# Computing the first MLP matrix product of the last chunk with seven block products instead of eight

## The chip, the core and the metric

The kernel runs on one core of a Trainium2 chip. The metric is the device time of one execution in microseconds (us); less is better. A core has a matrix engine (TensorE, PE in the profile; its weight loads are shown apart as PEld), a vector engine (VectorE, DVE), a scalar engine (ScalarE, ACT), a general engine (GpSimd, POOL) and SyncE (SP), which here only issues transfers. Each engine works through a queue of its own, in the order of the program, and waits for the others by semaphores. Matrix products land in eight PSUM banks of 512 float32 values in each of 128 partitions; everything else lies in SBUF.

## The reference, cut to what matters

```python
# retention: q, k, v are (4, 8, 768, 64)
for t in range(S):
    state = gamma * state + einsum('bhd,bhe->bhde', k[:, :, t], v[:, :, t])
    y[:, :, t] = scale * einsum('bhd,bhde->bhe', q[:, :, t], state)
x = y.transpose(0, 2, 1, 3).reshape(3072, 512)
# MLP: w_in is (512, 2048), w_out is (2048, 512)
h = x @ w_in
c = sqrt(2 / pi)
g = 0.5 * h * (1 + tanh(c * (h + 0.044715 * h**3)))
return g @ w_out
```

## The kernel before, in words

The 768 steps are cut into six chunks of 128 steps (0 to 5). For each chunk and each of four batches the attention part makes x, stored transposed as `xT[c]`: model dimension on the partitions (four tiles `kc` of 128), 4 x 128 tokens along the free axis. Then comes the MLP of these 512 tokens in two stages.

M1 is h = x @ w_in. `moe1(c, fc)` makes one of 16 tiles of 128 columns of w_in: `moe1_mm` (L348) runs four matmuls of 512 tokens, one for each `kc`, into an "h" bank, and `gelu` (L364) on ACT writes the tile in float16 to `g_sb`. There are two "h" banks, two "o" banks and four "att" banks.

M2 is g @ w_out. It is already done with seven products for eight. The 16 tiles are taken as eight pairs `fp` (r = 0 or 1 in a pair), the tokens as a half b = 0 or 1 (twice, a = 0 or 1), the outputs as halves x = 0 or 1. `g_sums` makes four sums of blocks of g (`s_g[1]` to `s_g[4]`), `w_sums` four of w_out (`t_w[1]` to `t_w[4]`), both through `tt` (L387). `PROD` lists seven products; `units_w(c)` runs them in 14 units, (product, a), each of eight matmuls of 256 columns (L456). X and Z name two banks. The partial sums are copied out between products (`SNAP`, to s_p, s_u, s_q, L479) and added to later banks on DVE (`ADD`, L387), and blocks of the output are stored. In the last chunk, 5, each half a has its own bank, X and Z in "o" and "h" banks, and the stores are cut finer.

```python
PROD = (
    ("X", (0, 0), (0, 0), True, False),
    ("Z", (1, 0), (1, 0), True, True),
    ("X", 2, 2, False, False),
    ("Z", 1, 1, True, False),
    ("X", 3, 3, False, False),
    ("Z", 4, (1, 1), False, True),
    ("X", (1, 1), 4, False, True),
)
```

A tuple names a block, a number one of the four sums; `True, False` say that a bank is begun and that it is ended.

The order on every engine is written out by hand. `run(units, after)` runs a list of units and after unit i what `after[i]` names. For chunks 2 to 5 the units are 16 of M1 and then 14 of M2 (so unit 16 is the first of M2). In between stand the attention work of the next chunk (n = c + 1), the loads of the one after (m = c + 2, issued by SP after unit 0), and the sums of g after units 3, 7, 11 and 15: on POOL in chunks 2 to 4, on DVE in chunk 5. In chunk 4 the attention of chunk 5 ends after unit 25.

The load buffers have tags "q32" and "k32" (eight each) and "v32" (six); each holds 2 KB in a partition. The whole of w_in lies in SBUF in four tiles `w_in_sb[0]` to `w_in_sb[3]`, of four `fc` each.

Of the kernel before, what the change touches and what calls it, by code (L numbers as in the profile page):

```python
# [9 lines left out]
F16 = mybir.dt.float16  # L10
F32 = mybir.dt.float32
AF = mybir.ActivationFunctionType
ALU = mybir.AluOpType
# [3 lines left out]
def kernel(  # L17
# [9 lines left out]
    nc = tc.nc  # L27
    B, H, S, Dh = q.shape
    C = 128
    NCk = S // C  # L30
# [3 lines left out]
    NF = d_ff // 128  # L34
# [23 lines left out]
    ld = ctx.enter_context(tc.tile_pool(name="ld", bufs=2 * B))  # L58
    pre = ctx.enter_context(tc.tile_pool(name="pre", bufs=2 * B))
    att = ctx.enter_context(tc.tile_pool(name="att", bufs=4))  # L60
    xp = ctx.enter_context(tc.tile_pool(name="xp", bufs=1))
    gp = ctx.enter_context(tc.tile_pool(name="gp", bufs=1))
# [27 lines left out]
    def load(c):  # L90
# [20 lines left out]
        out=misc[:, 0:1], in_=zero[:, 0:1], func=AF.Gelu_apprx_tanh, scale=1.0  # L111
# [15 lines left out]
    for j in range(2):  # L127
        for hp in range(NHP):
            nc.vector.tensor_scalar(
                out=mask[:, j, hp],  # L130
                in0=cst[:, OT:OT + 128],
# [8 lines left out]
    def copy_on(eng, out, in_):  # L140
        if eng is nc.scalar:
            eng.copy(out=out, in_=in_)  # L142
        else:
            eng.tensor_copy(out=out, in_=in_)
# [26 lines left out]
    xT = {}  # L171
# [4 lines left out]
    def bank(tag, dt=F32, shape=(128, NHP, 128), name="ps"):  # L176
        return psum.tile(list(shape), dt, tag=tag, bufs=BANKS[tag], name=name)
# [120 lines left out]
    def att_AY(c, bs, tag, ca, abs_, eng):  # L298
# [20 lines left out]
    w_in_sb = [  # L319
        const.tile([128, NHP, n * 128], F16, name=f"w_in{i}") for i, n in enumerate(w_in_n)  # L320
    ]
    w_in_of = {
        at + r: (i, r) for i, (n, at) in enumerate(zip(w_in_n, w_in_at)) for r in range(n)
    }
# [18 lines left out]
    g_sb = {}  # L343

    def moe1_mm(c, fc, out, t0, t1):
        wi, wr = w_in_of[fc]
        for kc in range(NHP):
            nc.tensor.matmul(  # L348
                out=out,
                lhsT=w_in_sb[wi][:, kc, wr * 128:(wr + 1) * 128],  # L350
                rhs=xT[c][:, kc, t0:t1],
                start=(kc == 0),
                stop=(kc == NHP - 1),
                skip_group_check=True,
            )

    def g_tile(c, fc):
        if (c, fc // 8) not in g_sb:
            g_sb[c, fc // 8] = gp.tile([128, 8, B * C], F16, tag=f"g{fc // 8}", name="g")
        r = fc % 8 // 2 * 2  # L360
        return g_sb[c, fc // 8][:, r:r + 2]

    def gelu(out, in_):
        nc.scalar.activation(out=out, in_=in_, func=AF.Gelu_apprx_tanh, scale=1.0)  # L364

    def moe1(c, fc):
        h_ps = bank("h", shape=(128, B * C), name="h_ps")
        moe1_mm(c, fc, h_ps, 0, B * C)
        gelu(g_tile(c, fc)[:, fc % 2], h_ps)
# [11 lines left out]
    s_g = {i: const.tile([128, NP, 2, C], F16, name=f"s_g{i}") for i in (1, 2, 3, 4)}  # L381
# [4 lines left out]
    def tt(eng, out, in0, in1, op):  # L386
        eng.tensor_tensor(out=out, in0=in0, in1=in1, op=op)  # L387
# [5 lines left out]
        tt(nc.vector, t[2], w_q(i, 1, 1), t[1], ALU.subtract)  # L393
        tt(nc.vector, t[4], w_q(i, 1, 0), t[2], ALU.subtract)

    def g_sums(eng, c, f0, f1, p0=0, p1=2):
        g = g_sb[c, f0 // 4].rearrange("p (f r) (a b t) -> p r b f a t", r=2, a=2, b=2)
        i = f0 % 4
        q = {
            (r, b): g[:, r, b][:, i:i + f1 - f0, p0:p1] for r in range(2) for b in range(2)  # L400
        }
        t = {j: s_g[j][:, f0:f1, p0:p1] for j in s_g}
        tt(eng, t[1], q[0, 1], q[1, 1], ALU.add)
        tt(eng, t[2], t[1], q[0, 0], ALU.subtract)
        tt(eng, t[3], q[0, 0], q[0, 1], ALU.subtract)
        tt(eng, t[4], q[1, 0], t[2], ALU.subtract)

    def lhs(c, key, fp, a):
        if key in s_g:
            return s_g[key][:, fp, a]  # L410
        r, b = key
        b = 2 * a + b
        return g_sb[c, fp // 4][:, 2 * (fp % 4) + r, b * C:(b + 1) * C]

    def rhs(key, fp):
        if key in t_w:
            return t_w[key][:, fp]
        r, x = key
        return w_out_sb[fp // 2][:, 2 * (fp % 2) + r, x * hw:(x + 1) * hw]

    PROD = (
        ("X", (0, 0), (0, 0), True, False),
# [7 lines left out]
    SNAP = {0: "s_p", 2: "s_u", 3: "s_q"}  # L434

    ADD = {1: (0, 0, "s_p"), 4: (1, 1, "s_q"), 5: (0, 1, "s_u")}

    def units_w(c):
        ps, o_sb, snap = {}, {}, {}
        last = c == NCk - 1  # L440

        def bank_of(k, a, new):
            if new:
                if last:
                    ps[k, a] = bank(("o", "h")[a], shape=(128, 2, hw), name="o_ps")[:, 0]
                else:
                    if a == 0:
                        ps[k] = bank("o", shape=(128, 2, hw), name="o_ps")
                    ps[k, a] = ps[k][:, a]
            return ps[k, a]  # L450

        def mm(n, a):
            k, lk, rk, new, stop = PROD[n]
            po = bank_of(k, a, new)
            for fp in range(NP):
                nc.tensor.matmul(  # L456
                    out=po,
                    lhsT=lhs(c, lk, fp, a),
                    rhs=rhs(rk, fp),
                    start=(new and fp == 0 and (last or a == 0)),  # L460
                    stop=(stop and fp == NP - 1),
                    skip_group_check=True,
                )

        def o_tile(b):
            if b not in o_sb:
                o_sb[b] = op.tile([128, 2, d_model], F32, tag=f"o{b}", name="o_sb")
            return o_sb[b]

        def snap_tile(nm):  # L470
            if nm not in snap:
                snap[nm] = op.tile([128, 2, hw], F32, tag=nm, name=nm)
            return snap[nm]

        def ev(n, a0, a1):
            k = PROD[n][0]
            p = ps[k, a0].unsqueeze(1) if last else ps[k]
            if n in SNAP:
                nc.scalar.copy(out=snap_tile(SNAP[n])[:, a0:a1], in_=p)  # L479
            elif n in ADD:  # L480
                b, x, nm = ADD[n]
                o = o_tile(b)[:, a0:a1, x * hw:(x + 1) * hw]
                tt(nc.vector, o, p, snap[nm][:, a0:a1], ALU.add)
            else:
                nc.scalar.copy(out=o_tile(1)[:, a0:a1, 0:hw], in_=p)  # L485

        def store(b, a0, a1, n0, n1, eng):
            rows = out.rearrange("(a b t) n -> b t a n", a=2, b=2)
            eng.dma_start(  # L489
                out=rows[b, c * C:(c + 1) * C, a0:a1, n0:n1], in_=o_sb[b][:, a0:a1, n0:n1]  # L490
            )

        def unit(n, a):
            mm(n, a)
            if not last:
                if a == 1:
                    ev(n, 0, 2)
                    if n > 4:
                        store(n - 5, 0, 2, 0, d_model, nc.gpsimd)
            elif n < 6:  # L500
                ev(n, a, a + 1)
                if n == 4 and a == 1:
                    store(1, 1, 2, hw, d_model, nc.sync)
                if n == 5:
                    store(0, a, a + 1, 0, d_model, (nc.scalar, nc.sync)[a])
            elif a == 0:
                ev(n, a, a + 1)
                store(1, 0, 1, 0, d_model, nc.scalar)
            else:
                nc.scalar.copy(out=o_tile(1)[:, 1, 0:hw], in_=ps["X", 1])  # L510
                store(1, 1, 2, 0, hw, nc.sync)

        return [(lambda n=n, a=a: unit(n, a)) for n in range(7) for a in range(2)]

    def units_0():
        ps, snap = {}, {}
# [91 lines left out]
    def run(units, after):  # L608
        for i, u in enumerate(units):
            u()  # L610
            for f, *args in after.get(i, ()):
                f(*args)

    VE, AC, PO, SY = nc.vector, nc.scalar, nc.gpsimd, nc.sync
# [173 lines left out]
    for c in range(2, NCk):  # L788
        n, m = c + 1, c + 2
        after = {} if n == NCk else {  # L790
            12: [(att_AY, n, (), "att", n, (0, 1), None)],
            19: [(att_AY, n, (0, 1), "h", n, (2, 3), VE)],
            22: [(att_S, n, 0, 1)],
            25: [(att_AY, n, (2, 3), "h", n, (), AC), (att_S, n, 2, 3)],
        }

        def more(at, *what):
            after[at] = after.get(at, []) + list(what)

        for i in range(4):  # L800
            at = 4 * i + 3
            after[at] = [(g_sums, PO if n < NCk else VE, c, 2 * i, 2 * i + 2)] + after.get(at, [])
        if m < NCk:
            more(0, (load, m))
            for b in range(B):
                more((18, 20, 23, 26)[b], (prep_qk, m, b))
                more(24, (prep1, PO, "v", m, b))
        run([(lambda fc=fc: moe1(c, fc)) for fc in range(NF)] + units_w(c), after)


# [28 lines left out]
```

## Time and profile before

| | |
|---|---|
| median of three timed runs | 207.29 us (206.85 to 207.32) |
| the profiled execution's own time | 206.68 us |
| its span, first to last instruction | 204.9 us |
| TensorE clock granted | 1.000 |
| PE busy | 196.4 us, 96% |
| DVE busy | 103.1 us, 50% |
| ACT busy | 102.2 us, 50% |
| POOL busy | 121.9 us, 60% |
| M1 of chunk 5, from the span's start | 175.23 to 189.17 us |
| M2 of chunk 5 | 189.17 to 201.60 us |

The span is what the trace covers; the 1.8 us between it and the execution's time lie around it. "Busy" is the time in which an engine worked on an instruction. Instructions of one engine overlap at their ends, so the mean length of one is more than its share of a dense row: a matmul of 256 columns is shown as 273 ns long while the next starts 109 ns after it. The timeline gives start, length, engine, line, operation and what it writes and reads, and in brackets the idle time ahead of it with what ended that. The chain of waits follows the last instruction back to what released each step.

### The profile page before, as it was taken

Reading aid. Unit: us, or ns where it says so; the run is one execution under the profiler, and the core shown is the slowest. Engines: PE = TensorE matmul, PEld = TensorE weight load, DVE = VectorE, ACT = ScalarE, POOL = GpSimd, SP = SyncE. Lnnn points to the kernel's source line nnn. Section 1 sums busy time; section 2 is a strip of 40 time slices with the busy share of each in tenths; the row PEclk is TensorE's granted clock in tenths of the full one; section 3 lists DMA queues with packets and bytes.
Section 4 is the critical chain, followed back from the end, with each engine's and each line's share of the span. In section 5 each row is a group of like instructions: output and inputs, shape, how many; then the busy total and the mean of one; then the engine's idle time right before and its main releaser. Section 6 shows DMA issues by size and latency. Waiting matters only on the chain.

```text
span 204.9 us, 4576 instructions
## 1 busy us (share of the span) xinstructions
PE 196.4 (96%) x1868; PEld 136.2 (66%) x1868; DVE 103.1 (50%) x239; ACT 102.2 (50%) x180; POOL 121.9 (60%) x124
## 2 busy tenths in 40 slices
PE   5798999999999999999999999999999999999993
PEld 1456747888687888644788644778644788544882
DVE  5346669679970459601379502289402284053420
ACT  2375464563479418466635365635366411566321
POOL 0599323944099999569997269996279980200000
PEclk9999999999999999999999999999999999999999
DMA  7999999999986899999982999442420000400004
GB/s 164 288 260 207 206 207 267 348 318 218 333 187 87 190 239 248 176 278 272 251 170 55 162 350 253 109 102 57 142 110 3 2 3 0 205 0 3 0 21 184
DMA packets 87092, 34.21 MB, mean 167 GB/s; under 512 B 80032, under 2 KB 84512, under 8 KB 87072
## 3 DMA queue, kind: packets, MB, share of 16 engines
q1 hardware_dynamic: 73920, 19.25, 44.0%
q0 software_dynamic: 6624, 12.58, 23.8%
q10 hardware_dynamic: 6528, 2.10, 4.1%
q8 instruction: 14, 0.23, 0.5%
q14 instruction: 6, 0.05, 0.1%
HBM read 27.63 MB, written 6.29 MB: 166 GB/s over the span
## 4 chain that ended last, share of the span: by engine, by line
PE 87%; DMA 7%; DVE 3%; ACT 1%; ACTq 1%; POOL 1%; issue 0%
PE h_ps L348 40%; PE o_ps L456 31%; DMA w_in<-in_moe_w_in_dram 4%; PE o_ps L525 3%; PE y_ps L242 3%; PE a_ps L207 3%; DMA k<-in_k_dram 3%; PE o_ps L558 2%; PE y_ps L229 2%; DVE st L285 2%; PE s_ps L266 1%; PE qkT_ps L187 1%; DVE a_sb L220 1%; ACT g L364 1%; ACTq L85 1%; POOL qk L158 1%
## 5 line engine op out<-in xcount | busy, mean ns | idle before, releaser
L348 PE MATMUL h_ps<-xT,w_in 128*128 128x512 f16 (+2 forms) x488 | 87.7, 334 | 0.5 <-ACT g L364 0.5
L364 ACT ACTIVATE g<-h_ps 128x512 f16<-128x512 f32 (+1 forms) x98 | 57.5, 589 | 33.1 <-PE h_ps L348 32.9
L348 PEld LDWEIGHTS <-w_in 128*128 128x128 f16 x488 | 45.4, 98 | 37.8 <-issue 2.2
L220 DVE TENSOR_TENSOR a_sb<-a_ps,mask 128x512 f16<-128x512 f32 x48 | 30.1, 683 | 43.7 <-PE a_ps L207 43.7
L387 POOL TENSOR_TENSOR s_g<-g 128x512 f16<-128x512 f16 x32 | 36.8, 1152 | 11.6 <-ACT g L364 11.6
L456 PEld LDWEIGHTS <-s_g 128*128 128x128 f16 x320 | 30.2, 98 | 4.7 <-POOL s_g L387 0.7
L456 PE MATMUL o_ps<-t_w,s_g 128*128 128x256 f16 x240 | 28.1, 273 | 0.0
L456 PEld LDWEIGHTS <-g 128*128 128x128 f16 x240 | 23.5, 98 | 3.6
L158 POOL TENSOR_TENSOR v<-v,cst 128x512 f16<-128x512 f32 x20 | 20.4, 1044 | 4.6 <-DMA v<-in_v_dram 3.7
L285 DVE SCALAR_TENSOR_TENSOR st<-st,cst,s_ps 64x128 f16<-64x128 f16 (+1 forms) x80 | 20.6, 318 | 0.7 <-PE s_ps L266 0.5
L387 POOL TENSOR_TENSOR s_g<-s_g,g 128x512 f16<-128x512 f16 x16 | 18.4, 1152 | 1.3
L387 POOL TENSOR_TENSOR s_g<-g,s_g 128x512 f16<-128x512 f16 x16 | 18.4, 1153 | 0.0
L456 PE MATMUL o_ps<-w_out,g 128*128 128x256 f16 x160 | 18.3, 273 | 0.0
L489 POOL DMA_DIRECT2D out_dram<-o_sb x8 | 5.9, 737 | 17.9 <-DVE o_sb L387 17.0
L258 DVE TENSOR_TENSOR xT<-y_ps,dec 128x512 f16<-128x512 f32 x20 | 13.0, 685 | 4.0 <-PE y_ps L242 3.8
L142 ACT CAST qk<-q 128x512 f16<-128x512 f32 x20 | 12.4, 620 | 2.9 <-DMA q<-in_q_dram 2.9
L387 DVE TENSOR_TENSOR s_g<-g 128x512 f16<-128x512 f16 x16 | 6.7, 421 | 11.8 <-ACT g L364 11.8
L485 ACT COPY o_sb<-o_ps 128x512 f32<-128x512 f32 (+1 forms) x5 | 2.7, 543 | 19.9 <-PE o_ps L456 17.6
L142 ACT CAST qk<-k 128x512 f16<-128x512 f32 x20 | 12.4, 620 | 0.4 <-DMA k<-in_k_dram 0.3
L387 DVE TENSOR_TENSOR o_sb<-o_ps,s_p 128x512 f32<-128x512 f32 (+1 forms) x7 | 4.3, 616 | 15.4 <-ACT qk L142 8.0
L479 ACT COPY s_u<-o_ps 128x512 f32<-128x512 f32 (+1 forms) x6 | 3.1, 514 | 17.2 <-PE o_ps L456 12.0
L456 PE MATMUL o_ps<-w_out,s_g 128*128 128x256 f16 x80 | 9.6, 273 | 0.0
(62 smaller groups left out, 179.9 us busy)
## 6 DMA issues: line engine op xcount, KB each, us to landing
out_dram<-o_sb POOLq DMA_DIRECT2D x10, 512.0 KB, 5.1
k<-in_k_dram SPq DMA_DIRECT2D x18, 256.0 KB, 4.2
q<-in_q_dram SPq DMA_DIRECT2D x18, 256.0 KB, 4.6
v<-in_v_dram SPq DMA_DIRECT2D x18, 256.0 KB, 4.5
w_in<-in_moe_w_in_dram POOLq DMA_DIRECT2D x4, 512.0 KB, 9.1
w_out<-in_moe_w_out_dram POOLq DMA_DIRECT2D x4, 512.0 KB, 14.4
q<-in_q_dram POOLq DMA_DIRECT2D x4, 256.0 KB, 11.3
k<-in_k_dram POOLq DMA_DIRECT2D x4, 256.0 KB, 9.6
```

What stands on the lines that cost most here:

```text
L142: eng.copy(out=out, in_=in_)
L158: eng.tensor_tensor(out=t, in0=src, in1=cst[:, col:col + H].unsqueeze(2).broadcast_to([128, H, Dh]), op=ALU.mult,)
L207: nc.tensor.matmul(out=ps[j][:, hp], lhsT=t[j * 64:(j + 1) * 64, 1, hp], rhs=t[j * 64:(j + 1) * 64, 0, hp], start=True, stop=True,)
L220: nc.vector.tensor_tensor(out=s, in0=ps[j], in1=mask[:, j], op=ALU.mult)
L242: nc.tensor.matmul(out=y_ps[j * 64:(j + 1) * 64, hp], lhsT=h16["v", c, b][:, 2 * hp + j], rhs=a_sb[c, b, j][:, hp], start=(c == 0), stop=True,
L258: nc.vector.tensor_tensor(out=x, in0=ps, in1=dec, op=ALU.mult)
L285: nc.vector.scalar_tensor_tensor(out=t[:, :, hp], in0=t[:, :, hp], scalar=cst[sl, OG + hp:OG + hp + 1], in1=s_ps[sl, :, hp], op0=ALU.mult, ...
L348: nc.tensor.matmul(out=out, lhsT=w_in_sb[wi][:, kc, wr * 128:(wr + 1) * 128], rhs=xT[c][:, kc, t0:t1], start=(kc == 0), stop=(kc == NHP - ...
L364: nc.scalar.activation(out=out, in_=in_, func=AF.Gelu_apprx_tanh, scale=1.0)
L387: eng.tensor_tensor(out=out, in0=in0, in1=in1, op=op)
L456: nc.tensor.matmul(out=po, lhsT=lhs(c, lk, fp, a), rhs=rhs(rk, fp), start=(new and fp == 0 and (last or a == 0)), stop=(stop and fp == NP ...
L525: nc.tensor.matmul(out=ps[k][:, a], lhsT=lhs(0, lk, fp, a), rhs=rhs(rk, fp), start=(first and fp == 0 and a == 0), stop=(stop and fp == NP ...
```

## The change

M1 of chunk 5 is done in the manner of M2. Pairs `pr` of tiles of w_in give r = 0, 1; the four tiles `kc` of the model dimension are halved (K = 0, 1); the tokens are halved as above. A group G is two pairs, 512 values of a bank, so there are four groups; each has seven products of four matmuls of 256 columns.

- `win_sums(i)` makes four sums of blocks of `w_in_sb[i]` on DVE. Two calls stand after units 0 and 1 of chunk 3, two after units 0 and 1 of chunk 4. The sums lie in buffers tagged "q32" and "k32".
- `x_sums(5)` makes four sums of blocks of `xT[5]` on DVE after unit 27 of chunk 4, in "v32" buffers.
- `units_h(5)` takes the place of the 16 `moe1` units. Each group has its X in an "att" bank, the first Z in an "h" bank, the second Z in an "o" bank. X is copied out after product 0 (on ACT) and product 2 (on DVE), Z after product 3 (on ACT for groups 0 and 2, on DVE for 1 and 3); DVE adds a bank to such a copy after products 1, 4 and 5. The gelu reads three of the four blocks from these copies in SBUF and the last from the bank.
- The sums of g of chunk 5 are parted: for pairs 0 and 1 and the first two sums of pairs 2 and 3 on POOL, the rest on DVE, the last six after unit 19.

```diff
+    def win_sums(i):
+        h, p0 = i // 2, i % 2 * 2
...
+        w = w_in_sb[i].rearrange("p (K k) (f r n) -> p K r k f n", K=2, r=2, n=128)
+        q = {(K, r): w[:, K, r] for K in range(2) for r in range(2)}
+        t = {j: t_in[j, h][:, :, p0:p0 + 2] for j in (1, 2, 3, 4)}
+        tt(nc.vector, t[1], q[0, 1], q[1, 1], ALU.add)
+        tt(nc.vector, t[2], t[1], q[0, 0], ALU.subtract)
+        tt(nc.vector, t[3], q[0, 0], q[0, 1], ALU.subtract)
+        tt(nc.vector, t[4], q[1, 0], t[2], ALU.subtract)
...
+    def x_sums(c):
...
+        tt(nc.vector, t[1], w[0, 1], w[0, 0], ALU.subtract)
+        tt(nc.vector, t[2], w[1, 1], t[1], ALU.subtract)
+        tt(nc.vector, t[3], w[1, 1], w[0, 1], ALU.subtract)
+        tt(nc.vector, t[4], w[1, 0], t[2], ALU.subtract)
...
+        def mm(G, n):
+            k, lk, rk, new, stop = PROD[n]
+            if new:
+                tag = "att" if k == "X" else "h" if n == 1 else "o"
+                ps[G, k] = bank(tag, shape=(128, 2, 2, 128), name="h_ps")
+            for p in range(2):
+                for kc in range(2):
+                    nc.tensor.matmul(
+                        out=ps[G, k][:, p],
+                        lhsT=lhs_h(lk, 2 * G + p, kc),
+                        rhs=rhs_h(rk, kc),
...
+        def keep(eng, G, n):
+            tag = {0: "q32", 2: "k32", 3: "v32"}[n]
+            t = ld.tile([128, 2, 2, 128], F32, tag=tag, bufs=6 if n == 3 else 8, name="h_sb")
+            copy_on(eng, t, ps[G, PROD[n][0]])
+            snap[G, SNAP[n]] = t
+
+        def add(G, n):
+            t = snap[G, ADD[n][2]]
+            tt(nc.vector, t, ps[G, PROD[n][0]], t, ALU.add)
+
+        def act(G, n):
+            r, col, nm = ADD.get(n, (1, 0, None))
...
+            gelu(
+                g[:, r, 1 - col][:, p0 % 4:p0 % 4 + 2],
+                snap[G, nm] if nm else ps[G, "X"],
+            )
...
+        def first(G):
+            mm(G, 0)
+            keep(A, G, 0)
+            mm(G, 1)
+            add(G, 1)
+
+        def second(G, eng):
+            mm(G, 2)
+            keep(V, G, 2)
+            mm(G, 3)
+            keep(eng, G, 3)
+
+        def third(G):
+            mm(G, 4)
+            add(G, 4)
+            mm(G, 5)
+            add(G, 5)
...
+        return [
+            lambda: first(0),
+            lambda: first(1),
+            lambda: (second(0, A), many((0, 1))),
+            lambda: (second(1, V), many((1, 1))),
+            lambda: third(0),
+            lambda: (third(1), many((0, 4), (0, 5))),
+            lambda: (mm(0, 6), many((0, 6), (1, 4))),
+            lambda: first(2),
+            lambda: mm(1, 6),
+            lambda: (first(3), many((1, 5), (1, 6))),
+            lambda: (second(2, A), many((2, 1))),
+            lambda: (second(3, V), many((3, 1))),
+            lambda: third(2),
+            lambda: (third(3), many((2, 4), (2, 5))),
+            lambda: (mm(2, 6), many((2, 6), (3, 4))),
+            lambda: (mm(3, 6), many((3, 5), (3, 6))),
+        ]
...
-        for i in range(4):
+        for i in range(4 if n < NCk else 0):
             at = 4 * i + 3
-            after[at] = [(g_sums, PO if n < NCk else VE, c, 2 * i, 2 * i + 2)] + after.get(at, [])
+            after[at] = [(g_sums, PO, c, 2 * i, 2 * i + 2)] + after.get(at, [])
+        if n == NCk:
+            t12, t34 = (1, 2), (3, 4)
+            after = {
+                7: [(g_sums, PO, c, 0, 2, 0, 2, t12)],
+                9: [(g_sums, PO, c, 2, 4, 0, 2, t12), (g_sums, PO, c, 0, 2, 0, 2, t34)],
+                15: [(g_sums, VE, c, 4, 6, 0, 2, t12), (g_sums, VE, c, 6, 8, 0, 2, t12)],
+                19: [(g_sums, VE, c, i, i + 2, 0, 2, t34) for i in (2, 4, 6)],
+            }
+        if c in (3, 4):
+            for i in range(2):
+                more(i, (win_sums, 2 * (c - 3) + i))
+        if c == 4:
+            more(27, (x_sums, n))
...
+        m1 = units_h(c) if n == NCk else [(lambda fc=fc: moe1(c, fc)) for fc in range(NF)]
+        run(m1 + units_w(c), after)
```

More of the change, by code (lines that the diff above doesn't have):

```diff
@@ L394, in w_sums, with g_sums @@
         tt(nc.vector, t[4], w_q(i, 1, 0), t[2], ALU.subtract)
-    def g_sums(eng, c, f0, f1, p0=0, p1=2):
+    def g_sums(eng, c, f0, f1, p0=0, p1=2, keys=(1, 2, 3, 4)):
         g = g_sb[c, f0 // 4].rearrange("p (f r) (a b t) -> p r b f a t", r=2, a=2, b=2)
@@ L402, in g_sums @@
         t = {j: s_g[j][:, f0:f1, p0:p1] for j in s_g}
[L403 to L406, printed above, removed]
+        ops = (
+            (1, q[0, 1], q[1, 1], ALU.add),
+            (2, t[1], q[0, 0], ALU.subtract),
+            (3, q[0, 0], q[0, 1], ALU.subtract),
+            (4, q[1, 0], t[2], ALU.subtract),
+        )
+        for j, in0, in1, o in ops:
+            if j in keys:
+                tt(eng, t[j], in0, in1, o)
     def lhs(c, key, fp, a):
@@ L419, in rhs, with x_blk @@
         return w_out_sb[fp // 2][:, 2 * (fp % 2) + r, x * hw:(x + 1) * hw]
+    t_in, s_x = {}, {}
+    def win_sums(i):
+        h, p0 = i // 2, i % 2 * 2
+        for j in (1, 2, 3, 4):
+            if (j, h) not in t_in:
+                t_in[j, h] = ld.tile([128, 2, 4, 128], F16, tag="qk"[h] + "32", bufs=8, name="t_in")
+        w = w_in_sb[i].rearrange("p (K k) (f r n) -> p K r k f n", K=2, r=2, n=128)
[5 more added lines that the diff above has]
+        tt(nc.vector, t[4], q[1, 0], t[2], ALU.subtract)
+    def x_blk(c, K, col):
+        x = xT[c].rearrange("p (K k) (a b t) -> p K b k a t", K=2, a=2, b=2)
+        return x[:, K, 1 - col]
+    def x_sums(c):
+        for i in range(2):
+            s_x[c, i] = ld.tile([128, 2, 2, 2, 128], F16, tag="v32", bufs=6, name="s_x")
+        t = {j: s_x[c, (j - 1) // 2][:, (j - 1) % 2] for j in (1, 2, 3, 4)}
+        w = {(K, x): x_blk(c, K, x) for K in range(2) for x in range(2)}
+        tt(nc.vector, t[1], w[0, 1], w[0, 0], ALU.subtract)
+        tt(nc.vector, t[2], w[1, 1], t[1], ALU.subtract)
+        tt(nc.vector, t[3], w[1, 1], w[0, 1], ALU.subtract)
+        tt(nc.vector, t[4], w[1, 0], t[2], ALU.subtract)
     PROD = (
@@ L513, in units_w, with units_h, lhs_h, rhs_h @@
         return [(lambda n=n, a=a: unit(n, a)) for n in range(7) for a in range(2)]
+    def units_h(c):
+        ps, snap = {}, {}
+        def lhs_h(key, pr, k):
+            if key in s_g:
+                return t_in[key, pr // 4][:, k, pr % 4]
+            K, r = key
+            wi, wr = w_in_of[2 * pr + r]
+            return w_in_sb[wi][:, 2 * K + k, wr * 128:(wr + 1) * 128]
+        def rhs_h(key, k):
+            if key in s_g:
+                return s_x[c, (key - 1) // 2][:, (key - 1) % 2, k]
+            return x_blk(c, *key)[:, k]
+        def mm(G, n):
[9 more added lines that the diff above has]
+                        rhs=rhs_h(rk, kc),
+                        start=(new and p == 0 and kc == 0),
+                        stop=(stop and kc == 1),
+                        skip_group_check=True,
+                    )
+        def keep(eng, G, n):
[8 more added lines that the diff above has]
+            r, col, nm = ADD.get(n, (1, 0, None))
+            p0 = 2 * G
+            if (c, p0 // 4) not in g_sb:
+                g_sb[c, p0 // 4] = gp.tile([128, 8, B * C], F16, tag=f"g{p0 // 4}", name="g")
+            g = g_sb[c, p0 // 4].rearrange("p (f r) (a b t) -> p r b f a t", r=2, a=2, b=2)
+            gelu(
+                g[:, r, 1 - col][:, p0 % 4:p0 % 4 + 2],
+                snap[G, nm] if nm else ps[G, "X"],
+            )
+        V, A = nc.vector, nc.scalar
+        def first(G):
[13 more added lines that the diff above has]
+            add(G, 5)
+        def many(*what):
+            for G, n in what:
+                act(G, n)
+        return [
[16 more added lines that the diff above has]
+        ]
@@ L798, in more @@
             after[at] = after.get(at, []) + list(what)
-        for i in range(4):
+        for i in range(4 if n < NCk else 0):
             at = 4 * i + 3
-            after[at] = [(g_sums, PO if n < NCk else VE, c, 2 * i, 2 * i + 2)] + after.get(at, [])
+            after[at] = [(g_sums, PO, c, 2 * i, 2 * i + 2)] + after.get(at, [])
[8 more added lines that the diff above has]
+        if c in (3, 4):
+            for i in range(2):
+                more(i, (win_sums, 2 * (c - 3) + i))
+        if c == 4:
+            more(27, (x_sums, n))
         if m < NCk:
@@ L807 @@
                 more(24, (prep1, PO, "v", m, b))
-        run([(lambda fc=fc: moe1(c, fc)) for fc in range(NF)] + units_w(c), after)
+        m1 = units_h(c) if n == NCk else [(lambda fc=fc: moe1(c, fc)) for fc in range(NF)]
+        run(m1 + units_w(c), after)
 _INS = ['q', 'k', 'v', 'moe_w_in', 'moe_w_out']
```

## The prediction, made before the changed kernel ran

> **What bounds the kernel now.** I read the page's busy shares first, then the chain of waits at its end, then the windows of the last two stages, then the timeline around chunk 5.
>
> ```profile
> PE 196.4 (96%) x1868; PEld 136.2 (66%) x1868; DVE 103.1 (50%) x239; ACT 102.2 (50%) x180; POOL 121.9 (60%) x124
> ```
>
> TensorE is the bound over the span. The share says nothing about the stage that changes, so next comes the end of the chain (start, length, what).
>
> ```profile
> 175.39 13.94 PE h_ps L348 x64
> 189.33 12.24 PE o_ps L456 x112
> 201.57 0.02 issue
> 201.59 0.37 ACT o_sb L510
> ```
>
> M1 of chunk 5 is 64 matmuls of 512 columns in 13.94 us, 217.8 ns each. M2 of chunk 5 is 112 matmuls of 256 columns in 12.24 us, 109.3 ns each. Neither waits, and the last copy and store hang on M2's end: a us that TensorE gains or loses here is a us of the kernel.
>
> ```profile
> 175.23:189.17 13.94, 13.94 (x67) 6.26 (x65) 4.57 (x12) 9.54 (x16) 0.90 (x2) 1.00 0.19 76
> 189.17:201.60 12.43, 12.39 (x113) 10.86 (x111) 4.07 (x10) 3.21 (x9) 0.00 (x0) 1.00 0.12 46
> ```
>
> In M1's window (stretch and its length; busy time of PE, PEld, DVE, ACT, POOL; clock; DMA) DVE is busy 4.57 us, ACT 9.54, POOL 0.90. That room is what the change spends. The prices of the new steps come from these timeline rows (start, length, engine):
>
> ```profile
> 126.88 2.48 DVE L220 TENSOR_TENSOR a_sb<-a_ps,mask 128x512 f16<-128x512 f32 x4 [11.53 <-PE a_ps L207]
> 131.60 0.58 ACT L479 COPY s_p<-o_ps 128x512 f32<-128x512 f32 x1 [1.21 <-PE o_ps L456]
> 132.09 0.62 ACT L142 CAST qk<-q 128x512 f16<-128x512 f32 x1
> 132.60 0.62 ACT L142 CAST qk<-k 128x512 f16<-128x512 f32 x1
> 39.26 0.59 ACT L536 COPY s_p<-o_ps 128x512 f32<-128x512 f32 x1 [1.77 <-PE o_ps L525]
> 39.88 0.69 DVE L387 TENSOR_TENSOR o_sb<-o_ps,s_p 128x512 f32<-128x512 f32 x1 [0.36 <-ACT s_p L536]
> 190.07 0.42 DVE L387 TENSOR_TENSOR s_g<-g 128x512 f16<-128x512 f16 x1 [1.83 <-ACT g L364]
> 190.59 0.42 DVE L387 TENSOR_TENSOR s_g<-s_g,g 128x512 f16<-128x512 f16 x1
> 119.41 1.14 POOL L387 TENSOR_TENSOR s_g<-g 128x512 f16<-128x512 f16 x1 [2.28 <-ACT g L364]
> ```
>
> A DVE operation on a bank of 512 f32 lasts 0.69 but the next may start 0.60 after it ((2.48 - 0.69)/3). An ACT copy from a bank lasts 0.59 and the next starts after 0.49; from SBUF 0.62 and 0.51. A result crosses engines in about 0.04 (39.85 to 39.88), in 0.10 where the operation has two waits (190.49 to 190.59), and reaches PE in 0.05.
>
> **The change, part by part.**
>
> *Matmuls.* 64 of 512 columns go; 4 groups x 7 products x 4 = 112 of 256 come. M2's row is that very form: 112 x 109.3 ns = 12.24. Saved: 13.94 - 12.24 = 1.70 us, if PE never waits. (The Trainium skill, TensorE: Matmul & The Clock Gate, Back-to-back issue gap, gives for streams with weight loads 81 ns at 128 and 131 ns at 512 columns; an estimate between them is 98 ns at 256, by which 112 x 98 - 64 x 131 would be a loss of 2.6 us. This trace has 217.8 and 109.3, so the measurement decides.)
>
> *Sums ahead.* `win_sums` is 2 x 4 DVE operations at the start of M1 of chunks 3 and 4. Four take 1.63 us (0.52 to the second, which needs the first, then 0.34, 0.34, and 0.42 for the last). DVE's last add of chunk 2 ends at 115.35 and its next work is at 126.88; eight end by 118.7, before POOL's first sum at 119.41. Cost nothing. Were POOL held back there, PE would feel most of it, since weight loads in M2 already wait 0.7 us in all for POOL's sums. `x_sums` is four more, from about 174.3 (behind the add at 173.68) to 175.9; before, DVE then idled until 179.64. It is first needed by product 2 of group 0 near 177. Nothing. No DMA is added; the new tiles borrow load buffers whose readers are done (chunk 4's q casts end at 110.8, SP issues the next q load at 113.07), so SP's queue waits for nothing new.
>
> *Sums of g.* Of 16 DVE sums of 0.42, eight go to POOL (8 x 1.11 = 8.9 us; POOL idles after 177.0), and six t3/t4 go behind M2's second product. POOL's are ready at about 189.4, DVE's t1/t2 at 191.3, wanted from 192.7; t3/t4 at 195.5, wanted at 196.2. Nothing, with 0.7 us of slack. No row has a two-input f16 DVE sum beside a POOL sum. (The Trainium skill, SBUF — State Buffer, Who interferes with whom, says that these two block one another for a whole instruction; DVE's sum at 188.9 would then start at 189.4, and the slack takes it.) Bounds from the rows: 0 to one POOL sum, 1.15; I take 0.
>
> *The banks.* New in M1: 12 DVE adds, 6 DVE copies and 6 ACT copies; the 16 gelus stay, 12 now reading SBUF. DVE: 18 x 0.60 = 10.8 us; ACT: 6 x 0.49 + 4 x 0.49 + 12 x 0.51 = 11.0. Both are under 12.24, but PE waits for them: a product that adds to X may not start until the copy of X before it is done. A late DVE operation delays PE, and behind PE the next bank. So I walked the queues in the order of `units_h`, from 175.23.
>
> First run: ACT's copy of X0 ends 176.5 (chunk 4's last copy holds ACT until 175.92), DVE's first add starts 176.61, and eight more follow at 0.60 from 177.43, ending 182.3. PE loses 0.04 and 0.05 in waits for two adds of group 0, and 0.05 for the like add of group 2 later: 0.14.
>
> The gap: ACT gets its second pair of gelus when DVE's adds end, at 180.55 and 181.15, does two more (181.66, 182.17), and only then copies group 2's X, 182.69 to 183.27. DVE has nothing for 1.06 us, and PE waits 0.14 for product 2 of group 2.
>
> Second run: nine DVE operations from 183.37 at 0.60; the eighth starts 187.56, the ninth 188.16. PE waits 0.24 for the copy at 184.57 to 185.26. It reaches group 3's last product at 187.54, but the eighth ends 188.25: 0.76. M1 ends at 175.23 + 12.24 + 1.27 = 188.74. Then M2 wants group 3's gelus as its seventh matmul at 189.39; ACT, five gelus behind (187.09, 187.69, 188.20, 188.72, 189.23), gives the one it needs at 189.84: 0.50.
>
> Waits: 0.14 + 0.14 + 0.24 + 0.76 + 0.50 = 1.78. **Sum: -1.70 + 1.78 = +0.08 us.** The profiled execution, 206.68, would become 206.76. It lies 0.61 below the median of the three timed runs, 207.29; the shift is the same on either: 207.4.
>
> **What the unknowns are worth** (each a total in place of +0.08). DVE spacing: the rows give 0.60 only for operations whose waits were long over; if each waited for the whole 0.69 before it, the walk gives +1.1. At 0.58 it gives -0.1, at 0.56 -0.35. ACT spacing at the whole 0.59: +0.7; at 0.46: -0.1. Hand-over at zero everywhere: -0.3; two-wait hand-overs of 0.15: +0.2. M2's matmuls might wait for a later gelu of the same tile than the one they read (the last ends 190.35, half a us later): +0.6. I keep the rows' values, since these are the same operations on the same shapes.
>
> **The rivals.**
>
> *Faster: the queues keep up.* With no waits the saving is whole: 207.29 - 1.70 = 205.6. For it: 10.8 and 11.0 us of work in 12.24. Against: the gap above, in which DVE waits for ACT and ACT for DVE. To gain over 0.62 us at least 40% of the waits must go, that is the 0.76, or the 0.50 and the 0.24. Halved waits give 206.5. Chance 0.18.
>
> *Slower: DVE is the bound of M1.* If chained adds start only after the one before has ended (as t1 to t2 do above, 0.52 for 0.42), 18 operations take 12.4 us plus the start of 1.4 and the gap: the walk's +1.1, 208.4. It decides from a spacing of 0.65. For it: nearly every add has two waits. Against: mixed DVE runs in the trace keep 0.60. The ACT row at 0.59 and the gelu of the same tile come to the same side, 207.9 to 208.0. Chance 0.35 for this side.
>
> *It does not do what it says:* `win_sums` holds POOL back in chunks 3 and 4, two DVE sums (0.7 us) in each, and M2 there waits for it: 207.4 + 1.4 = 208.8. Against: the 0.7 us between 118.7 and 119.41. In the chance above.
>
> **How the numbers follow.** About 0.3%, 0.62 us, is what a measurement of this kernel can tell from no change. Forecast (no change, 207.4; its own range 206.8 to 207.9) 0.47, faster 0.18, slower 0.35. The range of 8 in 10 goes from the halved waits, 206.4, to beyond the whole DVE length, 208.6.
>
> **What would show it.** In the changed profile: the new h_ps matmuls 109 ns apart; PE waits on DVE in the last 2 us before M2 and on ACT for its seventh matmul; a DVE gap of about 1 us in mid M1; M1 about 13.5 us, M2 about 12.7. Wrong if M1 takes under 12.9 (waits overrated) or over 14.1 (DVE spacing), if M2 waits for s_g, or if chunks 3 and 4 end later than 145.5 and 175.2.

## The result, and the profile after

| | before | change |
|---|---|---|
| median, six runs each | 207.31 us | 206.69 us |
| ratio, with 95% interval | | 0.9982 (0.9958 to 1.0007) |
| the same, a second time (17 and 12 runs) | 207.16 us | 207.09 us |
| ratio, with 95% interval | | 0.9994 (0.9971 to 1.0017) |
| profiled execution, its span | 206.68, 204.9 us | 206.68, 204.8 us |
| M1 of chunk 5, first matmul to M2's first | 13.94 us | 13.34 us |
| M2, first matmul to the end of the last one's turn | 12.23 us | 12.74 us |

No change that a measurement of this kernel can tell; forecast was 207.4 us and no change. (The ratios and their intervals come from all the runs and not from the two medians, so they differ a little from the medians' quotient.) The first median, 206.69, lies 0.1 us under the range that the prediction gave for no change (206.8 to 207.9), the second, 207.09, inside it; both lie in its range of 8 in 10. M1 and M2 of chunk 5 together went from 26.17 to 26.08 us. PE works less and waits more. First the page's busy row of the changed kernel, and the windows of its M1 and M2 (stretch, its length, then busy time of PE, PEld, DVE, ACT and POOL, clock, DMA):

```profile
PE 194.6 (95%) x1916; PEld 140.4 (69%) x1916; DVE 119.5 (58%) x271; ACT 104.3 (51%) x186; POOL 129.0 (63%) x130
```

```profile
175.18:188.51 13.33, 12.72 (x114) 10.92 (x112) 11.52 (x20) 10.67 (x21) 6.93 (x8) 1.00 0.20 80
188.51:201.43 12.92, 12.57 (x114) 10.78 (x111) 6.86 (x17) 4.20 (x11) 0.81 (x1) 1.00 0.12 45
```

PE's busy time fell by 1.8 us and the span by 0.1. In M1, DVE (4.57 before) now works 11.52 of 13.33 us, ACT 10.67. PE, which filled its stage before, is no longer busy through it. The chain of waits of the changed kernel's end shows who holds it (start, length, what):

```profile
175.34 2.63 PE h_ps L571 x24
...
182.65 0.48 ACT h_sb L142
...
183.76 0.69 DVE h_sb L387
...
184.50 0.60 ACT h_sb L142
185.10 1.06 ACT g L364 x2
186.16 0.68 DVE h_sb L387
186.84 0.02 issue
186.86 2.76 ACT g L364 x5
189.62 0.05 issue
189.67 11.76 PE o_ps L490 x106
201.43 0.02 issue
201.45 0.37 ACT o_sb L544
```

Before, this stretch was two pieces of PE. Now the chain leaves PE at 178.0 and returns to it only at 189.67: in between it passes from ACT to DVE and back, over copies and adds of banks (h_sb) and the gelus that read them. The timeline of the changed kernel has the waits themselves, in brackets:

```profile
175.86 0.59 ACT L142 COPY h_sb<-h_ps 128x512 f32<-128x512 f32 x1
176.48 1.51 DVE L387 TENSOR_TENSOR h_sb<-h_ps,h_sb 128x512 f32<-128x512 f32 x2 [0.70 <-ACT h_sb L142]
...
180.42 1.23 ACT L364 ACTIVATE g<-h_sb 128x512 f16<-128x512 f32 x2 [0.73 <-DVE h_sb L387]
182.55 1.06 ACT L142 COPY h_sb<-h_ps 128x512 f32<-128x512 f32 x2
183.15 1.29 DVE L387 TENSOR_TENSOR h_sb<-h_ps,h_sb 128x512 f32<-128x512 f32 x2 [0.98 <-ACT h_sb L142]
184.36 1.88 DVE L144 COPY h_sb<-h_ps 128x512 f32<-128x512 f32 x3
186.15 2.47 DVE L387 TENSOR_TENSOR h_sb<-h_ps,h_sb 128x512 f32<-128x512 f32 x4
188.08 0.60 PE L571 MATMUL h_ps<-s_x,w_in 128*128 128x256 f16 x4 [0.60 <-DVE h_sb L387]
188.17 1.16 POOL L387 TENSOR_TENSOR s_g<-g,s_g 128x512 f16<-128x512 f16 x1
188.51 0.82 PE L490 MATMUL o_ps<-w_out,g 128*128 128x256 f16 x6
188.68 0.92 DVE L387 TENSOR_TENSOR s_g<-g 128x512 f16<-128x512 f16 x1
189.67 3.01 PE L490 MATMUL o_ps<-w_out,g 128*128 128x256 f16 x26 [0.34 <-ACT g L364]
```

DVE stands idle for 0.98 us until ACT has copied the bank of group 2; then its nine operations run without a pause from 183.15 to 188.6; the last product of group 3 waits for the eighth of them, and the seventh matmul of M2 for the five gelus that ACT began when the sixth ended (186.84). (The bracket counts from the modelled end of a matmul. From start to start the gaps beyond a matmul's 0.109 us are 0.12 and 0.18 us before products 2 and 4 of group 2, 0.76 before the last product of group 3 and 0.50 in M2; 0.02 and 0.05 stand before product 6 of groups 0 and 2.) None of the prediction's signs of being wrong came: M1 took 13.34 us, no matmul of M2 waited for a sum of g, and chunks 3 and 4 ended at 145.43 and 175.18.

### The profile page after: what moved, and what is told of

It reads as the page before. It is cut to its first block, busy times and chain, and to the rows that moved or that the text cites. A ratio compares the mean times of both kernels' runs of the same rounds, so it can differ in the third digit from the quotient of the medians.

```text
span 204.8 us, 4729 instructions
## 1 busy us (share of the span) xinstructions
PE 194.6 (95%) x1916; PEld 140.4 (69%) x1916; DVE 119.5 (58%) x271; ACT 104.3 (51%) x186; POOL 129.0 (63%) x130
## 4 chain that ended last, share of the span: by engine, by line
PE 81%; ACT 5%; DVE 4%; DMA 3%; POOL 3%; SPq 1%; issue 1%; DVEq 0%; ACTq 0%
PE h_ps L348 33%; PE o_ps L490 30%; ACT g L364 4%; PE o_ps L654 3%; DMA k<-in_k_dram 3%; PE y_ps L242 3%; PE a_ps L207 3%; PE o_ps L687 2%; PE y_ps L229 2%; DVE st L285 2%; POOL qk L158 2%; PE s_ps L266 1%; PE h_ps L571 1%; POOL w_in L329 1%; DVE h_sb L387 1%; PE qkT_ps L187 1%
## 5 line engine op out<-in xcount | busy, mean ns | idle before, releaser
L348 PE MATMUL h_ps<-xT,w_in 128*128 128x512 f16 (+2 forms) x424 | 73.6, 327 | 0.5 <-ACT g L364 0.5
L364 ACT ACTIVATE g<-h_ps 128x512 f16<-128x512 f32 (+1 forms) x86 | 50.3, 588 | 29.3 <-PE h_ps L348 29.0
L348 PEld LDWEIGHTS <-w_in 128*128 128x128 f16 x424 | 39.1, 98 | 30.4 <-issue 1.8
L387 POOL TENSOR_TENSOR s_g<-g 128x512 f16<-128x512 f16 x35 | 40.3, 1152 | 16.9 <-ACT g L364 16.8
L387 POOL TENSOR_TENSOR s_g<-s_g,g 128x512 f16<-128x512 f16 x18 | 20.8, 1153 | 1.4
L387 POOL TENSOR_TENSOR s_g<-g,s_g 128x512 f16<-128x512 f16 x17 | 19.6, 1154 | 0.0
L490 PE MATMUL o_ps<-t_w,g 128*128 128x256 f16 x80 | 9.5, 273 | 0.0
```

The source lines that it names most:

```text
L348: nc.tensor.matmul(out=out, lhsT=w_in_sb[wi][:, kc, wr * 128:(wr + 1) * 128], rhs=xT[c][:, kc, t0:t1], start=(kc == 0), stop=(kc == NHP - ...
L490: nc.tensor.matmul(out=po, lhsT=lhs(c, lk, fp, a), rhs=rhs(rk, fp), start=(new and fp == 0 and (last or a == 0)), stop=(stop and fp == NP ...
```

## The experiments

The theory, W: the 1.70 us are saved, and PE's waits for copies, adds and gelus of the banks take them back; the waits come from the order in which the queues are written (O), not from DVE and ACT being too slow for the work. Rivals: the new matmuls gain little by themselves (P); ACT, not DVE, sets the end (A); the work cannot be laid beside 12.24 us of PE in any order (T). The profiled executions differ by up to 1 us in when chunk 5 starts, in the first 50 us of the kernel, so lengths are given from the first matmul of its M1 (e6, where chunks 3 and 4 grew, starts chunk 5 later still); the medians stand beside runs of the kernel before on the same chip.

| kernel | M1, us | M2, us | median, us | before, us | ratio (95%) |
|---|---|---|---|---|---|
| change | 13.34 | 12.74 | 206.69 | 207.31 | 0.9982 (0.9958 to 1.0007) |
| change again (e10) | 13.35 | 12.74 | 207.09 | 207.16 | 0.9994 (0.9971 to 1.0017) |
| e2 no copies or adds | 12.23 | 13.03 | 206.03 | 207.13 | 0.9949 (0.9934 to 0.9965) |
| e8 same, gelus reordered | 12.23 | 12.23 | 205.17 (one run) | 206.76 | |
| e3 two more on DVE | 14.54 | 12.74 | 207.96 | 207.13 | 1.0057 (1.0039 to 1.0076) |
| e4 two fewer on DVE | 12.78 | 12.74 | 206.50 | 207.13 | 0.9975 (0.9956 to 0.9993) |
| e7 two gelus exchanged | 13.35 | 12.41 | 206.55 | 206.76 | 0.9986 (0.9964 to 1.0009) |
| e5 new order | 12.23 | 12.45 | 205.46 | 207.13 | 0.9930 (0.9912 to 0.9947) |
| e9 new order, same engines | 12.23 | 12.23 | 205.19 | 207.16 | 0.9911 (0.9881 to 0.9941) |
| e1 sums ahead alone | 13.94 | 12.23 | 206.85 | 206.76 | 1.0006 (0.9987 to 1.0025) |
| e6 sums beside POOL | 13.35 | 12.74 | 218.34 (two runs) | 206.76 | 1.0556 (1.0489 to 1.0623) |

**Is the saving there? (e2, e8)**

```diff
         def keep(eng, G, n):
...
-            t = ld.tile(...)
-            copy_on(eng, t, ps[G, PROD[n][0]])
-            snap[G, SNAP[n]] = t
+            snap[G, SNAP[n]] = mask[:, 0].rearrange("p (x a) t -> p x a t", a=2)
...
         def add(G, n):
-            t = snap[G, ADD[n][2]]
-            tt(nc.vector, t, ps[G, PROD[n][0]], t, ALU.add)
+            pass
```

> Left out: the 12 copies and 12 adds between the products of M1 of chunk 5; three of the four blocks of g there are made from a constant in SBUF. The 112 matmuls and 16 gelus stay. Theory W (the saving of 1.70 us is there and the waits of PE for DVE and ACT eat it): M1 of chunk 5 takes 12.24 us, M2 12.24, and the time is 1.7 us under the kernel before, about 205.6. Rival P (PE itself gains little from the short matmuls with a split moving operand): M1 stays above 13 us and the time within 0.4 us of the kernel before.

M1 took 12.23 us, as theory W had it; rival P is out: 112 split matmuls of 256 columns cost the 109.3 ns of M2's. But the kernel gained 1.10 us by the medians, not 1.7, for M2 now waits 0.80 us. Its chain:

```profile
175.47 11.80 PE h_ps L571 x108
187.28 0.02 issue
187.30 1.64 ACT g L364 x3
188.94 0.05 issue
188.99 11.76 PE o_ps L490 x106
```

The expectation overlooked that three gelus stand in a row behind product 6 of group 2, and M2's seventh matmul wants the third. So this wait is there with no bank work at all. (Gelu (G, n) makes the block of g that product n of group G completes.) Next, gelu (3, 5) is put ahead of them:

```diff
-            lambda: (mm(2, 6), many((2, 6), (3, 4))),
-            lambda: (mm(3, 6), many((3, 5), (3, 6))),
+            lambda: (mm(2, 6), many((3, 5), (2, 6))),
+            lambda: (mm(3, 6), many((3, 4), (3, 6))),
```

> Left out as before: the copies and adds of M1 of chunk 5, with three of four blocks of g made from a constant. Gelu (3, 5) now stands ahead of (2, 6) and (3, 4). Theory W: the 0.80 us that was still waited in M2 goes, M1 and M2 take 12.2 us each, 1.7 us under the kernel before. Rival (M2 waits for something else): 0.8 us remain.

```profile
175.49 12.23 PE h_ps L571 x112
187.71 12.24 PE o_ps L490 x112
```

No wait is left: 24.46 us for both stages against 26.17 before, 1.71 less. The saving of 1.70 us is whole where nothing waits, and M2's wait was a place in ACT's queue.

**Which engine sets the end? (e3, e4)** In e3 the copies after product 3 of groups 0 and 2 go to DVE, in e4 those of groups 1 and 3 to ACT.

```diff
e3:
-            lambda: (second(0, A), many((0, 1))),
-            lambda: (second(2, A), many((2, 1))),
+            lambda: (second(0, V), many((0, 1))),
+            lambda: (second(2, V), many((2, 1))),
e4:
-            lambda: (second(1, V), many((1, 1))),
-            lambda: (second(3, V), many((3, 1))),
+            lambda: (second(1, A), many((1, 1))),
+            lambda: (second(3, A), many((3, 1))),
```

> The copies of Z after product 3 of groups 0 and 2 go from ACT to DVE: DVE 20 bank operations, ACT 4. Theory D (DVE's run of bank operations at 0.60 us each sets the end of M1): two more in line, about 1.2 us over the changed kernel, so 1.1 us over the kernel before. Rival A (ACT's queue sets it): two copies of 0.49 less on ACT, up to 1.0 us under the changed kernel.

> The copies of Z after product 3 of groups 1 and 3 go from DVE to ACT: DVE 16 bank operations, ACT 8. Theory D: the walk of the queues with the measured spacings gives 0.7 us under the changed kernel, 0.8 under the kernel before. Rival A: two copies of 0.49 more on ACT, up to 1.0 us over the changed kernel.

M1 grew by 1.20 us in e3, two operations of 0.60, and fell by 0.56 in e4. By the medians that is 0.83 us over and 0.63 us under the kernel before, where 1.1 and 0.8 were expected. Rival A is out: it has both signs the other way. The chains' last pieces ahead of M2 show the change of hands, first e3, then e4:

```profile
186.66 0.68 DVE h_sb L144
187.34 0.61 DVE h_sb L387
187.95 0.02 issue
187.98 2.76 ACT g L364 x5
```

```profile
185.92 0.47 ACT h_sb L142
186.39 3.19 ACT g L364 x6
189.58 0.05 issue
189.63 11.76 PE o_ps L490 x106
```

With two more operations DVE is on the chain to 187.95; with two fewer ACT holds all of the end. In e4 less was won (0.56) than two operations are worth (1.20): ACT takes over at once. Each is near its limit in the written order.

**The wait in M2 alone (e7)**

```diff
-            lambda: (mm(2, 6), many((2, 6), (3, 4))),
-            lambda: (mm(3, 6), many((3, 5), (3, 6))),
+            lambda: (mm(2, 6), many((2, 6), (3, 5))),
+            lambda: (mm(3, 6), many((3, 4), (3, 6))),
```

> Gelus (3, 5) and (3, 4) change places, so that ACT makes first what the seventh matmul of M2 reads. Theory (the 0.50 us wait there is the place in ACT's queue, not ACT's load): the walk gives 0.33 us under the changed kernel, the wait falls from 0.50 to 0.1 or 0.2. Rival (ACT is full there): no change.

The wait fell from 0.50 to 0.17 us and M2 from 12.74 to 12.41, 0.33 less, as the walk had it. The medians are too close to tell 0.33 us; the profile settles this one. So of the 1.6 us of waits 0.33 lie in the order of two gelus.

**The order as a whole (e5, e9)** The steps of `units_h` are written as one list: m is a matmul group, k a copy (A on ACT, V on DVE), a an add, g a gelu, s a sum of g (P on POOL, V on DVE); then group and product, or group and sum. e9's list, in which every step has the engine that it has in the change:

```diff
+        ORDER = """
+            m10 k10A m00 k00A m11 m13 a11 k13V m01 m02 k02V m30 m12 a01 m03 m15 k30A g11 m20
+            k12V m04 a15 k03A a04 g01 m05 m14 g15 k20A m23 a05 m32 a14 g04 m06 m33 k32V g05
+            k23A m22 m16 g06 k33V k22V s03P m34 m25 a34 m24 s01P g14 m21 g16 a25 g34 s11P
+            m35 s02P m36 g25 a24 m31 g24 a35 a21 m26 a31 g35 g36 g21 g26 g31 s21V s31V s22V
+            s12P s04P s32V
+        """
```

All four groups are begun early, product 5 of a group may come before product 4, and product 1 of group 3, which only one gelu reads, comes last but one. In e5 the list is like this, but eight of the twelve copies are on ACT and four on DVE (the expectation speaks of six), so that DVE has 16 bank operations.

> The same matmuls, copies, adds, gelus and sums as the changed kernel in another order of the queues: products of the four groups interleaved so that a bank has rested before it is added to, product 1 of group 3 last; 6 of 12 copies on ACT each way, as far as the walk wants. Theory W with the order as cause: the walk gives no wait of PE at all, M1 12.24 us, M2 12.24, 1.7 us under the kernel before, about 205.6. Rival T (DVE's 10.8 us and ACT's 11.0 us of bank work cannot be laid beside 12.24 us of PE in any order, because of hand-overs): at most 0.5 us under the kernel before.

> Order alone: every copy, add and sum on the engine that it has in the changed kernel (DVE 18 bank operations, ACT 6 copies), only their order and that of the products is new. Theory O (the order makes the waits): no wait of PE in the walk, M1 and M2 12.2 us each, 1.5 to 1.7 us under the kernel before. Rival S (the gain of the first new order came from moving two copies to ACT, as when that is done alone): about 0.7 us under it.

e5 is 1.67 us under the kernel before by the medians, e9 1.97, and their profiles have M1 of 12.23 us. Rivals T and S are out. The end of e9's chain, and its two windows:

```profile
176.25 12.23 PE h_ps L574 x112
188.48 12.24 PE o_ps L490 x112
200.72 0.02 issue
200.74 0.37 ACT o_sb L544
```

```profile
176.09:188.32 12.23, 12.23 (x115) 10.96 (x113) 11.07 (x19) 9.87 (x19) 5.30 (x6) 1.00 0.22 87
188.32:200.70 12.38, 12.38 (x114) 10.86 (x111) 6.93 (x18) 4.70 (x12) 2.33 (x3) 1.00 0.12 46
```

PE does not wait once, beside 11.07 us of DVE work and 9.87 of ACT work: the same operations on the same engines that cost 1.6 us of waits in the written order. e9 beats both kernels. Its 24.46 us are 1.71 less than before; that the median gave 1.97 is within the interval (0.9881 to 0.9941). In e5, M2 took 12.45 us with two gaps of 0.1, where weight loads wait for DVE's sums of g; the first of these starts only at 190.8, after a gelu:

```profile
192.23 0.11 PEld L490 LDWEIGHTS <-s_g 128*128 128x128 f16 x2 [0.21 <-DVE s_g L387]
192.56 1.42 PEld L490 LDWEIGHTS <-s_g 128*128 128x128 f16 x14 [0.22 <-DVE s_g L387]
```

> The changed kernel once more, beside the order. If its M1 and M2 together are 0.1 us shorter than before, the time is 0.1 us under the kernel before, within the noise.

The change beside e9: 207.09 against 207.16, the second pair of medians above; M1 and M2 together 26.09 us, 0.08 less than before.

**What the sums ahead cost (e1, e6)** In e1 only `win_sums` and `x_sums` stay, and M1 and the sums of g are those of before.

```diff
...
+            after = {4 * i + 3: [(g_sums, VE, c, 2 * i, 2 * i + 2)] for i in range(4)}
...
-        m1 = units_h(c) if n == NCk else [(lambda fc=fc: moe1(c, fc)) for fc in range(NF)]
+        m1 = [(lambda fc=fc: moe1(c, fc)) for fc in range(NF)]
```

> Of the change only the sums ahead stay (win_sums in chunks 3 and 4, x_sums in chunk 4); M1 of chunk 5 and its sums of g are those of the kernel before. Theory H (DVE's idle time hides them all): within 0.2 us of the kernel before, chunks 3 and 4 of the same length to 0.05 us. Rival (they cost part of the saving): up to 1.4 us slower, in the weight loads that wait for POOL's sums.

0.09 us over the kernel before, in the noise; chunk 3 takes 30.51 us from M1 to M1 (30.47 before), chunk 4 29.75 (29.76). Hidden. In e6 they run beside POOL's sums:

```diff
-                more(i, (win_sums, 2 * (c - 3) + i))
+                more(13, (win_sums, 2 * (c - 3) + i))
```

> The calls of win_sums stand after unit 13 of chunks 3 and 4, behind DVE's masks of unit 12, so that they run beside POOL's sums of g. Theory B (two-input f16 sums of DVE and POOL block one another, as one DVE sum of 0.92 us beside a POOL sum in the changed kernel suggests): the eight sums take up to 8 x 1.15 = 9 us in place of 3.3, DVE's additions and x of the next chunk come late, and each of chunks 3 and 4 grows by 1 to 5 us. Rival N (they do not block): eight sums in 3.3 us, ending before DVE's next add at 133.4, no change of the time.

The timeline of e6 in chunk 3, DVE first, then POOL:

```profile
130.48 0.70 DVE L387 TENSOR_TENSOR t_in<-w_in 128x512 f16<-128x512 f16 x1
131.21 1.26 DVE L387 TENSOR_TENSOR t_in<-t_in,w_in 128x512 f16<-128x512 f16 x1
132.39 1.37 DVE L387 TENSOR_TENSOR t_in<-w_in 128x512 f16<-128x512 f16 x1
...
138.86 1.37 DVE L387 TENSOR_TENSOR t_in<-w_in,t_in 128x512 f16<-128x512 f16 x1
140.15 0.68 DVE L387 TENSOR_TENSOR o_sb<-o_ps,s_p 128x512 f32<-128x512 f32 x1
```

```profile
128.62 1.17 POOL L387 TENSOR_TENSOR s_g<-g,s_g 128x512 f16<-128x512 f16 x1
129.73 1.17 POOL L387 TENSOR_TENSOR s_g<-g 128x512 f16<-128x512 f16 x1
130.97 1.22 POOL L387 TENSOR_TENSOR s_g<-s_g,g 128x512 f16<-128x512 f16 x1
132.15 1.33 POOL L387 TENSOR_TENSOR s_g<-g 128x512 f16<-128x512 f16 x1
```

Eight sums took 9.75 us (130.48 to 140.23), one for each sum of POOL, whose own grew from 1.17 to up to 1.34; in e1 the same eight, with no sum of POOL beside them, take 0.42 each and 3.0 us in all. DVE's add of M2 came 6.8 us later than in the kernel before (133.35 there, 140.15 here, of which 1.2 is e6's later start). Chunk 3 grew by 6.7 us and chunk 4 by 4.7, 11.6 us together by the medians. Theory B, and more than its 1 to 5 us: everything behind the sums in DVE's queue is late, and PE with it (4.4 us in two waits for DVE's o_sb, 1.3 for POOL's s_g). The place of `win_sums` in the first 4 us of M1, with POOL still waiting for gelus, is what keeps its price at nothing.

## Why the prediction was right, point by point

- *The saving of 1.70 us.* Right: 12.23 us for 112 matmuls in e2, e5, e8 and e9. The figures of the Trainium skill (TensorE: Matmul & The Clock Gate, Back-to-back issue gap) for streams with weight loads, from which the prediction estimated a loss of 2.6 us, do not hold in this kernel: 217.8 ns at 512 and 109.3 at 256 columns. The 217.8 is a mean. In the trace of the kernel before, the matmuls of M1 start 216 ns apart, but for two pauses of 0.07 us (before the 9th and the 41st), so 0.13 of the 1.70 us are pauses of the old M1 and not a lower price of the new products; "neither waits" passed over them.
- *The waits, 1.78 us.* Measured 1.62 (26.08 against 24.46 us): 0.12 for 0.14 at product 2 of group 2, 0.18 for 0.24 at product 4, 0.76 for 0.76 at the last product of group 3, 0.50 for 0.50 in M2; of the 0.14 in short waits 0.07 were left. The misses have one sign, 0.16 us together, which is why the sum was +0.08 where -0.09 came. Part of it is the hand-over: the prediction let an add start 0.10 us after ACT's copy, and in the change it started 0.03 after (176.45 to 176.48, 183.12 to 183.15). The row behind the 0.10 (190.49 to 190.59) is of another kind: DVE waits there for its own sum. A sum of g in the change does start 0.10 after the gelu that it waits for (188.58 to 188.68). What the hand-over alone is worth, no run measured.
- *DVE's run of operations at 0.60, with the gap for ACT.* Right in place and size: idle 0.98 us for 1.06, the second run from 183.15 for 183.37. e3 and e4 show that it is DVE that sets M1's end in the written order, with ACT just behind.
- *ACT's five gelus ahead of M2.* Right in size. The prediction did not part the late adds from the place in ACT's queue; e2 and e7 show that the order of the gelus alone is worth 0.33 us of the 0.50.
- *Nothing for the sums.* Right by e1, and by e6 only as long as they miss POOL's. The prediction counted eight sums of g for POOL; the change gives it six and DVE ten. Its times came out all the same: POOL's last ended at 189.33, for 189.4. In the change one DVE sum of g ran beside POOL's last (188.68 and 188.17 above) and took 0.92 us for 0.42, and the slack in M2 took it. That agrees with the skill (SBUF — State Buffer, Who interferes with whom).
- *The rivals.* "The queues keep up" did not happen in the change, but e9 shows that they can, with 205.2 us where it gave 205.6: the prediction weighed it by the length of the waits in the written order, and a new order takes them all away. "DVE at its whole length" did not happen: operations with two waits still followed one another at 0.60 (three copies in 1.88 us, four adds in 2.47).

## What to carry to other kernels

An algorithm with fewer products pays for them with copies and adds between products on the same bank; totals of 11 us on DVE and ACT beside 12 us of PE say only that it can fit. Walk the queues in order with start-to-start spacings and hand-overs from the trace: here that gave each wait to within 0.1 us, and, run over other orders, an order without any. Hide two-input DVE sums where POOL is not summing too.

## What the runs showed of the hardware that was not expected

That two-input f16 sums of DVE and POOL hold one another up was expected of e6. Its rows show more: they took turns one by one, DVE's 0.42 us became 1.26 to 1.37, and POOL, too, was slowed, from 1.17 to up to 1.34. DVE's adds of a bank to a copy in SBUF, beside POOL's sums in the change (186.15 to 188.6), kept their 0.68 us and their spacing of 0.60.
